# Linear attention into a Sinkhorn-routed mixture on one core: the emission table re-sorted, two small PSUM outputs moved within their bank

## The chip, the cores and the metric

The kernel runs on one core of a Trainium2 chip, in one launch. The metric is the device time of that core in microseconds (us), as the median of a few runs. Engines are named as the profile names them: PE multiplies matrices (PEld loads its weights), DVE and ACT work elementwise, POOL works elementwise and issues DMAs, SP issues DMAs. PSUM is the memory that PE writes to; it is cut into banks of 512 fp32 columns, and DVE and ACT read it.

## The reference

Linear attention over 8 batches, 8 heads, 576 positions and 64 dims, then an 8-expert layer whose routing weights come from Sinkhorn scaling. Cut to what matters:

```python
phi = lambda x: np.where(x > 0, x, np.exp(x) - 1.0) + 1.0
kv = einsum('bhsd,bhse->bhde', phi(k), v);  z = phi(k).sum(2)
att = einsum('bhsd,bhde->bhse', phi(q), kv) / (einsum('bhsd,bhd->bhs', phi(q), z)[..., None] + 1e-6)
x = att.transpose(0, 2, 1, 3).reshape(4608, 512)          # N = 4608 tokens
logits = x @ w_gate;  P = np.exp(logits - logits.max())   # N x 8
for _ in range(8):                                        # Sinkhorn
    P /= P.sum(1, keepdims=True) + 1e-9
    P /= P.sum(0, keepdims=True) + 1e-9                   # column sums over all tokens
    P *= N / E
out = sum over e of P[:, e:e+1] * (np.maximum(x @ w1[e], 0) @ w2[e])
```

## The kernel before, in words

**Work and stages.** Three stages overlap. The front makes attention for 16 pairs of batch and head group and writes `xT` (dims on partitions, tokens along the free side). The first expert, e = 0, starts as soon as tokens are there: 9 groups `g` of 512 tokens, each `relu(x @ w1) @ w2`. The other seven experts follow group by group (`unit`). From group 5 of expert 0 on, the first layer is done by `block7`, a seven-product scheme: for each half (`pair(0)`, `pair(1)`) PE makes products m1 to m7, each 4 matmuls 256 columns wide. Products m5 and m3 of a pair write one bank of the tile `att` ("att" in the profile), the others write `hq` and `Zye`. ACT copies parts of these products out (L767, L774, L781), DVE adds two of them and clips at zero (`addrelu`, the custom DVE instruction of L790, output `h`), ACT clips the other two (L784, L787). `unit_plain` then multiplies `h` by `w2` (L861, output `ye`).

**Sinkhorn.** While PE works on expert 0, DVE runs the 8 iterations of `sinkhorn`. One iteration is a chain of three steps: `f_a` on DVE (multiply, row sum, reciprocal, multiply, partial column sum `gs`; L503 to L510), `f_c` on PE (one small fp32 matmul with a matrix of ones, L515, which sums `gs` over the partitions into 8 columns of an `att` bank), `f_d` on DVE (`Dc` from those 8 columns, L519 the first time and L522 later, then a reciprocal, L524). The next `f_a` needs `f_d`. So does PE's next `f_c`, through the chain.

**Who shares what.** `att` is one PSUM tile `at2` of two banks. `att_bank()` hands out the banks in turn, for the router logits, for Sinkhorn's column sums and for the R bank of each `block7` pair:

```python
at2 = aps.tile([P, 2, 512], FP32, tag="att", name="att")
def att_bank():
    return at2[:, (len(p_att["order"]) - 1) % 2]
```

**What sets the order.** Each piece of work is a step with a number, added with its engine, a planned duration, dependencies and buffers. `_Plan.run` then calls the steps one after the other, and each call records its instructions. The first 1201 calls are written out by hand in `_FRONT` (a number, and a letter for the engine: p PE, a ACT, d DVE, g POOL, s SP, m a DMA's landing, n no engine). The rest is chosen greedily by planned time. The method `at` gives the planned start of a step on an engine; engine "none" stands for steps that only take a buffer. Every engine runs its own instructions in the order in which they were recorded.

**Where waits come from.** The recording layer adds the semaphore waits. When an instruction is recorded, it is made to wait for instructions of other engines recorded earlier whose accesses to the same tile conflict with its own. For `att` the programs show that it takes the two banks as one. In the program of before, the step that reads 8 column sums from columns 512 to 519 (second bank) waits for a matmul that writes columns 256 to 511 (first bank). Such a wait is called a cross-bank wait below. Its direction follows from the order of recording alone: the later recorded of the two waits. So the place of a step in `_FRONT` counts even between steps of different engines.

**Steps that the prediction names.** Sinkhorn's `f_c` are 512, 515, 518, 521, 524, 527, 530 and 533, its `f_d` are 513, 516 and so on to 534. 766, 780, 922, 988 and 1088 are m5 products, that is the first matmuls into an `att` bank; 767 is the ACT copy (L781) of 766's bank. 981 and 1052 are `f_h12`, the DVE step (L790) that reads a pair's finished `att` bank.

Of the kernel before, what the change touches and what calls it, by code (L numbers as in the profile page):

```python
# [17 lines left out]
class _Plan:  # L18
# [35 lines left out]
    def run(self):  # L54
# [10 lines left out]
        cfg = [0]  # L65

        def at(e, t, r):
            return max(free[e] + (self.TURN if e == "pe" and t["cfg"] != cfg[0] else 0.0), r)

        def slot(t):  # L70
# [64 lines left out]


_FRONT = """
    1n 2p 3p 4p 5p 102g 103m 6p 7p 8p 9p 10p 11p 12p 13p 14p 15p 16p 17p 18p 19p 20p 21p 117n 48s 49m 50g 51m 52g 53m
    75g 76m 106n 79g 80m 77g 78m 55d 54a 56d 124g 125m 0g 61n 126g 127m 62p 57n 22p 23p 24p 63a 107g 108m 64d 58p 59a
    65d 81a 25p 26p 27p 60d 66p 109g 110m 82d 83d 84n 28p 29p 151g 152m 111n 67a 153g 154m 88n 30p 31p 32p 68p 69a  # L140
    85p 86d 87a 89p 128g 129m 131d 71p 90a 70a 33p 583n 112g 113m 91d 34p 155g 156m 92d 114g 115m 35p 130a 36p 37p
    38p 39p 40p 41p 42p 43p 93p 44p 45p 72d 178g 179m 73p 74d 94a 46p 95p 96a 100p 137n 47p 116n 97a 132d 138p 584p
    180g 181m 182g 183m 585p 586p 587p 158d 101d 139a 98p 140d 99d 157a 164n 159d 165p 166a 133n 134p 135a 141d 118g
    119m 121g 122m 167d 588p 123n 160n 589d 590p 205g 206m 591d 168d 207g 208m 592p 136a 142p 161p 143a 144p 594p
    209g 210m 162d 234g 235m 236g 237m 145a 163d 596p 120n 169p 185d 146a 147p 597d 598p 600p 170a 171p 184a 148d
    599d 595d 149p 172a 602p 186d 191n 187n 238g 239m 192p 150d 188p 603d 593a 193a 606p 604p 189d 104g 105m 194d
    195d 173a 190a 176p 196p 177d 261g 262m 601a 605p 607p 612d 197a 211a 212d 213d 198p 174p 199a 608p 263g 264m
    200a 218n 219p 290g 291m 265g 266m 175d 220a 214n 221d 222d 215p 216a 620n 621p 217a 623p 622d 201p 292g 293m
    223p 202d 609p 241d 240a 614a 224a 624a 203p 225p 204d 625p 247n 226a 228p 227a 317g 318m 626a 232p 233a 267a
    627p 242d 243n 229d 248p 230p 629p 610p 268d 231d 244p 249a 250d 251d 296a 274n 319g 320m 344g 345m 630d 297d  # L150
    628a 616a 269d 275p 276a 277d 245a 611p 631p 321g 322m 270n 633p 278d 246a 252p 271p 632d 323a 253a 254p 272d
    346g 347m 634a 635p 641p 255a 273d 324d 653n 325d 348g 349m 371g 372m 256a 279p 280a 257p 258d 618d 654p 281p
    259p 303n 636a 655d 656p 282a 283a 294g 295m 260d 304p 284p 642p 305a 639p 657d 298d 285d 286p 306d 330n 649a
    331p 332a 287d 326n 307d 299n 300p 377a 402g 403m 301d 350a 658p 302d 333d 351d 660p 308p 327p 661d 334d 309a
    310p 328d 659a 311a 640p 400g 401m 378d 373g 374m 312a 662p 329d 315p 431g 432m 335p 352d 316d 664p 336a 313p
    337p 314d 637p 427g 428m 647a 338a 569d 663d 638p 357n 340p 358p 339a 341d 643p 359a 665d 342p 481g 482m 384n
    666p 360d 353n 343d 385p 361d 354p 386a 404g 405m 355a 645a 668p 356a 387d 644p 669a 362p 667d 570d 687p 363a
    670p 367p 364p 689p 456g 457m 651a 375g 376m 686n 672p 379d 571d 688a 365a 366a 406a 388d 368d 691p 548d 673p
    369p 370d 692a 407d 288p 680a 380n 381p 408d 413n 289a 433a 414p 676p 382d 572s 573m 415a 409n 454g 455m 549d
    487a 690a 383d 434d 416d 671p 677p 417d 555d 389p 410p 390a 391p 435d 693p 411d 429g 430m 412d 392a 393a 396p  # L160
    678d 550d 418p 419a 695p 397d 674p 420p 483g 484m 556d 557d 558s 559m 421a 394p 675p 395d 461d 440n 441p 694d
    696d 422a 436n 442a 437p 697p 699p 438d 458g 459m 485g 486m 439d 425p 443d 698a 398p 701p 426d 700a 444d 399a
    445p 423p 424d 488d 684a 682a 446a 460a 467n 720p 447p 452p 489d 703p 490g 448a 705p 462d 468p 702d 449a 719n
    463n 453d 706p 469a 450p 722p 470d 721a 538n 451d 495n 724p 496p 497a 551s 552m 471d 464p 704p 498d 560s 561m
    723a 465a 491n 466a 725d 726p 713d 574s 575m 499d 472p 473a 492p 493a 727d 474p 475a 494a 562d 563d 728p 476a
    711d 709p 500p 477p 576d 478d 501a 729d 710p 502p 503a 504a 479p 480d 707p 708p 505p 506d 730p 717d 577d 731d
    732p 507p 742p 508d 539g 540m 536n 756d 715a 734p 578d 763n 733a 757d 735d 752d 758d 759s 760m 509p 753d 754d
    736p 737p 510a 755d 537p 744a 511d 764p 808d 541g 542m 740p 778p 765a 553s 554m 768p 743p 543n 750d 770p 741p
    969s 970m 761s 762m 512p 769a 513d 748d 766p 771a 809d 810d 774p 544n 779a 780p 767a 781a 738p 772p 775d 514d
    784p 776p 786p 782p 785a 773d 579s 580m 788p 777a 787d 816p 783a 817a 739p 811s 812m 820p 789d 822p 515p 746a  # L170
    818p 790p 796p 819a 564d 565s 566m 567s 568m 516d 824p 517d 798p 823a 815n 799p 825d 797p 821a 518p 860d 791a
    830p 832p 806d 831a 826p 519d 861d 520d 836p 794p 837a 581s 582m 862d 827d 833a 1026s 1027m 804a 795p 840p 834p
    792p 841d 828p 829a 838p 839d 835a 793p 802d 868p 521p 870p 522d 842p 813s 814m 869a 800d 843a 523d 867n 545g
    546m 874p 912d 913d 871a 872p 873a 882p 863s 864m 846p 876p 883a 875a 888p 886p 889a 878p 524p 877d 848p 884p
    879d 885a 849p 847p 525d 854a 887a 914d 890p 880p 526d 547n 892p 850p 881a 893d 891d 527p 920p 856a 894p 844p
    895a 851p 845p 922p 858a 528d 529d 530p 852d 921a 926p 924p 927a 898p 923a 934p 928p 896p 919n 925a 915s 916m
    917s 918m 930p 935a 961d 531d 940p 941a 532d 899p 962d 897p 938p 906a 902p 929d 533p 931d 936p 937a 904a 534d
    939a 535d 944p 932p 942p 751a 943d 945d 745d 963d 903p 910d 933a 900p 865s 866m 946p 615d 972p 901p 954p 947a
    964d 973a 650d 974p 960n 978p 955p 908d 619d 975a 948p 965d 966d 959a 949p 979a 980p 976p 982p 681a 950p 971n
    613d 951p 652d 983d 648a 984p 986p 977a 956d 985a 987a 988p 952p 989a 992p 994p 967d 981d 968d 993a 995d 990p  # L180
    996p 1029p 712d 1031p 991a 1030a 714d 997d 953p 957d 998p 911d 1035p 1028n 1032a 1037p 958d 999a 1033p 1004p
    1000d 1036a 1005a 1006p 1001d 1009p 1039p 1034a 1002d 1003d 1014p 1007d 1008d 1040d 1010a 1012a 1038d 1015d 617a
    1016d 855d 1083s 1084m 679a 1017p 1041p 1043p 1045p 1020p 1044a 1046a 1049p 1051p 1042a 1022d 1047p 1050a 1021d
    1053p 1086p 646d 1048a 1088p 1018d 1052d 1054d 1087a 1023p 909d 1025d 1089a 1013g 1055p 1085n 1056a 1019d 1092p
    1093a 1024d 1094p 1011g 1057d 1090p 1061p 1058d 1063p 1062a 1066p 1059d 1064d 1065d 1060d 1096p 1097d 1140s 1141m
    718a 1091a 1095d 1067a 1068g 685d 1071p 1074p 1098p 1100p 1099a 1101a 1102p 1072d 1073d 1103a 1077p 1075d 1106p
    1107a 1108p 1104p 1110p 1143p 1078d 1145p 1079d 1069a 1080p 1105a 1142n 1070g 1111d 1144a 1112p 1109d 1149p 683a
    1146a 1082d 1197s 1198m 1113a 1076d 1081d 1114d 1115d 1116d 1117d 1150a 1151p 747d 1147p 1118p 1119a 1120p 1122d
    1121d 1123p 1153p 1154d 1128p 1131p 1155p 1157p 1159p 1130d 1133d 1124a 1129d 1152d 716a 1148a 749d 1158a 1160a
    1134p 1163p 1136d 1165p 1135d 1132d 1156a 1164a 1166d 1126a 1161p 1167p 1168d 1162a 1127g 1200p 1201a 1202p 1137p  # L190
    1203a 1169p 1170a 1139d 1138d 1206p 1207a 1208p 1204p 1175p 1171d 1172d 1176a 1177p 1180p 1199n 1205a 1173d 1174d
    1210p 1185p 1178d 1179d 1125g 1211d 1181a 1187d 1186d 1254s 1255m 1209d 1188p 1212p 1214p 1216p 1213a 1191p 1215a
    1217a
"""


@with_exitstack
def kernel(
    ctx: ExitStack,
    tc: tile.TileContext,  # L200
    q: bass.AP,
    k: bass.AP,
    v: bass.AP,
# [14 lines left out]
    NJ = S // PW  # L218
# [250 lines left out]
    def logits(b2):  # L469
        gl = S_.grp(p_att)  # L470

        def f_l(_):
            gl["tile"] = att_bank()[:, 0:NJ * E].rearrange("p (j e) -> p j e", e=E)
            for i in range(NJ):
                for c in range(NDT):
                    nc.tensor.matmul(gl["tile"][:, i, :], lhsT=xT[:, c, ts(NJ * b2 + i, P)], rhs=wg_sb[:, c, :],
                                     start=(c == 0), stop=(c == NDT - 1))
# [33 lines left out]
            gc = S_.grp(p_att)  # L511

            def f_c(_, gc=gc):
                gc["tile"] = att_bank()[:, 0:E]
                nc.tensor.matmul(gc["tile"], lhsT=ones_t, rhs=gs, start=True, stop=True)  # L515

            def f_d(_, it=it, gc=gc):
# [593 lines left out]
```

## Time and profile before

| | |
|---|---|
| median of 3 runs | 980.89 us (978.53, 980.89, 982.26) |
| the profiled execution's own time | 979.57 us |
| its span, first to last instruction | 977.8 us |
| PE busy | 959.2 us (98%), 8624 matmuls |
| DVE busy | 774.7 us (79%), 1481 instructions |
| ACT busy | 566.0 us (58%), 1004 instructions |
| POOL busy | 145.2 us (15%), 209 instructions |
| chain that ended last, by engine | PE 87%, DVE 6%, DMA 4%, ACT 1%, issue 1%, POOL 1% |
| column-sum matmuls (L515) | 8, each shown as two, 135.5 to 185.6 us |

PE's busy share holds little room, but a busy share tells nothing of the clock that PE was granted, and its gaps are not spread evenly. The bracket behind a row of the timeline is the idle time of the engine just before it and what ended that idle time. [...]

### The profile page before, as it was taken

To read this page: it belongs to the slowest core of one execution; us is meant where nothing else is said; L and a number is where in the kernel's file an instruction comes from. 1 tells how busy PE (TensorE), PEld (TensorE's weight loads), DVE (VectorE), ACT (ScalarE), POOL (GpSimd) and SP (SyncE) were. 2 spreads that over 40 slices of the span, in tenths; PEclk is the share of its full clock that TensorE was granted. 3 is DMA by queue.
4 is the path that set the end of the run, shared out by engine and by line. 5 is a ranking of instruction groups with operands and counts; after the bars stand their busy time and mean duration, and the time that the engine had idled before them with its cause. 6 is when DMAs were issued, how large, how long until landed. Compare 5 with 4: busy or idle time off the path is not lost.

```text
span 977.8 us, 21138 instructions
## 1 busy us (share of the span) xinstructions
PE 959.2 (98%) x8624; PEld 796.0 (81%) x8624; DVE 774.7 (79%) x1481; ACT 566.0 (58%) x1004; POOL 145.2 (15%) x209
## 2 busy tenths in 40 slices
PE   8999999899999999999999999999999999999998
PEld 4555566578888888888888888888888888888886
DVE  5897887778888788878888788878888788877775
ACT  6887744456555555555555555555555555555553
POOL 6441100001112111121112111121112111111110
PEclk9999999999999999999999999999999999999999
DMA  9997864012725422272225422272224422235554
GB/s 218 263 214 166 167 184 153 1 40 77 161 76 124 115 76 77 76 162 77 77 76 125 114 76 77 76 163 77 76 76 124 115 77 76 76 99 162 162 163 108
DMA packets 46193, 112.52 MB, mean 115 GB/s; under 512 B 4368, under 2 KB 26640, under 8 KB 46096
## 3 DMA queue, kind: packets, MB, share of 16 engines
q1 hardware_dynamic: 21056, 75.57, 23.6%
q0 software_dynamic: 24640, 35.07, 19.0%
q8 instruction: 67, 1.10, 0.4%
q10 hardware_dynamic: 400, 0.52, 0.2%
q14 instruction: 30, 0.25, 0.1%
HBM read 119.69 MB, written 17.69 MB: 141 GB/s over the span
## 4 chain that ended last, share of the span: by engine, by line
PE 87%; DVE 6%; DMA 4%; ACT 1%; issue 1%; POOL 1%; DVEq 0%; ACTq 0%; POOLq 0%
PE ye L979 32%; PE hq L755 23%; PE att L755 12%; PE Zye L755 6%; PE Zye L979 5%; PE ye L861 4%; DMA vv<-in_v_dram 2%; PE hq L633 2%; DMA w<-in_moe_w_dram 1%; DVE h L790 1%; DMA qin<-in_q_dram 1%; PE kv_ps L382 1%; PE att L409 1%; PE num_ps L432 0%; DVE W L919 0%
## 5 line engine op out<-in xcount | busy, mean ns | idle before, releaser
L993 DVE SCALAR_TENSOR_TENSOR acc<-ye,P_sb,acc 128x256 f32<-128x256 f32 x620 | 267.5, 479 | 124.8 <-PE ye L979 124.1
L755 PEld LDWEIGHTS <-W 128*128 128x128 f16 x2144 | 209.9, 98 | 29.7 <-issue 2.8
L979 PEld LDWEIGHTS <-S 128*128 128x128 f16 x1984 | 194.0, 98 | 23.9 <-DVE S L952 1.4
L1003 POOL TENSOR_TENSOR acc<-acc,st 128x256 f32<-128x256 f32 x124 | 88.0, 729 | 710.9 <-ACT st L1000 583.4
L979 PE MATMUL ye<-T,S 128*128 128x256 f16 x1488 | 192.8, 273 | 0.2 <-DVE S L952 0.2
L755 PEld LDWEIGHTS <-w 128*128 128x128 f16 x1608 | 157.7, 98 | 22.8 <-issue 2.8
L787 ACT ACTIVATE h<-hq 128x512 f16<-128x512 f32 x134 | 80.1, 598 | 150.9 <-PE hq L755 147.7
L979 PEld LDWEIGHTS <-h 128*128 128x128 f16 x1488 | 145.6, 98 | 17.4 <-issue 0.5
L755 PE MATMUL att<-xs,W 128*128 128x256 f16 x1008 | 151.2, 273 | 0.9 <-DVE h L790 0.8
L755 PE MATMUL hq<-xs,W 128*128 128x256 f16 x1008 | 151.2, 273 | 0.0
L755 PE MATMUL hq<-xs,w 128*128 128x256 f16 x1008 | 140.9, 273 | 0.9 <-DVE h L790 0.9
L784 ACT ACTIVATE h<-Zye 128x512 f16<-128x512 f32 x134 | 80.1, 598 | 40.1 <-PE Zye L755 40.1
L790 DVE CUSTOM_DVE_ANT_0 h<-att,s 128x512 f16<-128x512 f32 x126 | 86.6, 687 | 14.9 <-ACT s L774 10.0
L1000 ACT ACTIVATE st<-Zye,P_sb 128x256 f32<-128x256 f32 x124 | 52.3, 470 | 76.2 <-PE Zye L979 76.1
L952 DVE TENSOR_TENSOR S<-h 128x1024 f16<-128x1024 f16 x124 | 85.2, 687 | 10.9 <-ACT h L787 10.9
L774 ACT COPY s<-hq 128x512 f32<-128x512 f32 x126 | 73.5, 583 | 35.2 <-PE hq L755 35.1
L767 ACT COPY Zye<-hq 128x512 f32<-128x512 f32 x134 | 77.8, 581 | 25.5 <-PE hq L755 25.5
L790 DVE CUSTOM_DVE_ANT_0 h<-hq,s 128x512 f16<-128x512 f32 x126 | 86.6, 687 | 3.3 <-PE hq L755 3.0
L861 PE MATMUL ye<-w,h 128*128 128x512 f16 x312 | 76.8, 382 | 0.0
L781 ACT COPY s<-att 128x512 f32<-128x512 f32 x126 | 74.5, 591 | 3.4 <-PE att L755 2.3
L755 PE MATMUL Zye<-xs,w 128*128 128x256 f16 x504 | 75.6, 273 | 0.0
L979 PE MATMUL ye<-w,S 128*128 128x256 f16 x496 | 64.3, 273 | 0.7 <-DVE S L952 0.7
(102 smaller groups left out, 947.4 us busy)
## 6 DMA issues: line engine op xcount, KB each, us to landing
xs<-xd SPq DMA_DIRECT2D x63, 896.0 KB, 4.6
kin<-in_k_dram POOLq DMA_DIRECT2D x15, 576.0 KB, 8.5
out_dram<-acc SPq DMA_DIRECT2D x67, 128.0 KB, 2.4
w<-in_moe_w_dram POOLq DMA_DIRECT2D x16, 512.0 KB, 8.8
w<-in_moe_w_dram POOLq DMA_DIRECT2D x7, 1024.0 KB, 13.1
qin<-in_q_dram POOLq DMA_DIRECT2D x16, 288.0 KB, 7.4
vv<-in_v_dram POOLq DMA_DIRECT2D x16, 288.0 KB, 7.7
xd<-acc SPq DMA_DIRECT2D x5, 512.0 KB, 3.7
```

The costliest lines, as they stand in the source:

```text
L755: nc.tensor.matmul(dst[:, p, :], lhsT=lhs(p, c), rhs=rhs(c), start=(first and p == 0 and c == 0), stop=(c == 1), skip_group_check=True)
L767: nc.scalar.copy(out=Zt[1], in_=gX["tile"])
L774: nc.scalar.copy(out=gs2["tile"], in_=gX["tile"])
L781: nc.scalar.copy(out=gs5["tile"], in_=gR["tile"])
L784: nc.scalar.activation(out=hd(0, 0), in_=Zt[1], func=AF.Relu)
L787: nc.scalar.activation(out=hd(1, 0), in_=gX["tile"], func=AF.Relu)
L790: nc.vector._custom_dve(TENSOR_ADD_SAT, out=dst, in0=ps, in1=sb, s0=3.0e38, s1=0.0)
L861: nc.tensor.matmul(gy[tt]["tile"], lhsT=gh["tile"][:, f, ds(P * tt, P)], rhs=gw2["tile"][:, f, :], start=(f == 0), stop=(f == NFT - 1))
L952: nc.vector.tensor_tensor(out=Sx[:, i], in0=a0, in1=a1, op=op)
L979: nc.tensor.matmul(bank(g_)[:, s, :], lhsT=lhs(s, kk), rhs=rhs(kk), start=(new and s == 0 and kk == 0), stop=(kk == 3), skip_group_check=True)
L993: nc.vector.scalar_tensor_tensor(out=dst(), in0=bank(g_)[:, s, :], scalar=P_sb[:, gg, e:e + 1], in1=dst(), op0=ALU.mult, op1=ALU.add)
L1003: nc.gpsimd.tensor_tensor(out=dst(), in0=dst(), in1=gst["tile"], op=ALU.add)
```

## The change

Three edits.

1. In `_Plan.run`, `at` returns the ready time for engine "none", so that buffer-only steps no longer queue behind each other in the plan.
2. The logits and the column sums are written 16 fp32 columns further into their bank (columns 16 on, in place of 0 on).
3. The 1201 entries of `_FRONT` are put in another order, that of their planned times. The sequence of each engine's own entries (p, a, d, g, s) stays exactly as it was; what changes is how the engines' sequences are interleaved, and the places of some m and n entries.

```diff
         def at(e, t, r):
+            if e == "none":
+                return r
             return max(free[e] + (self.TURN if e == "pe" and t["cfg"] != cfg[0] else 0.0), r)
...
-            gl["tile"] = att_bank()[:, 0:NJ * E].rearrange("p (j e) -> p j e", e=E)
+            gl["tile"] = att_bank()[:, 2 * E:2 * E + NJ * E].rearrange("p (j e) -> p j e", e=E)
...
-                gc["tile"] = att_bank()[:, 0:E]
+                gc["tile"] = att_bank()[:, 2 * E:3 * E]
```

The new order, shown where the prediction uses it (stretches of the table, one step's neighbours each):

```
Sinkhorn's first column sums, 512p, their reader 513d, and the m5 products behind them
 before: 512p 769a 513d 748d 766p 771a 809d 810d 774p 544n 779a 780p 767a
 after:  512p 766p 513d 774p 767a 748d 780p
the sixth, 527p and 528d
 before: 527p 920p 856a 894p 844p 895a 851p 845p 922p 858a 528d 529d 530p
 after:  527p 891d 920p 894p 528d 844p 529d 895a 851p 845p 858a 921a 922p 852d 919n 530p
after Sinkhorn, the R bank's reader 981d and the next pair's m5, 988p
 before: 988p 952p 989a 992p 994p 967d 981d
 after:  981d 986p 985a 988p
and once more, 1052d and 1088p
 before: 1088p 1018d 1052d 1054d
 after:  1052d 1088p
```

Laid side by side, the two programs hold the same instructions in the same order on each of the five engines. Apart from the column offset they differ in the semaphores waited for by 39 instructions, 13 on PE, 16 on DVE and 10 on ACT. With edit 2 alone, no wait differs from before.

More of the change, by code (lines that the diff above doesn't have):

```diff
@@ L137 @@
 _FRONT = """
[L138 to L192, printed above, removed]
+    1n 102g 103m 117n 106n 583n 48s 49m 2p 3p 50g 51m 4p 52g 53m 5p 6p 75g 76m 7p 8p 79g 80m 9p 10p 77g 78m 55d 54a
@@ new lines @@
+    11p 12p 124g 125m 13p 14p 15p 0g 16p 56d 17p 18p 126g 127m 19p 20p 21p 61n 107g 108m 62p 109g 110m 22p 63a 23p
+    24p 57n 151g 152m 58p 64d 65d 25p 59a 26p 81a 27p 153g 154m 60d 82d 66p 28p 29p 67a 83d 30p 128g 129m 31p 32p 68p
+    84n 85p 69a 88n 112g 113m 89p 86d 87a 90a 71p 131d 155g 156m 33p 34p 35p 70a 36p 91d 37p 38p 114g 115m 39p 40p
+    92d 130a 41p 42p 43p 72d 93p 178g 179m 44p 94a 45p 73p 46p 74d 137n 95p 111n 180g 181m 96a 132d 100p 47p 97a 138p
+    182g 183m 158d 584p 139a 101d 585p 586p 118g 119m 157a 587p 140d 98p 99d 164n 165p 133n 121g 122m 159d 134p 166a
@@ new lines @@
+    141d 205g 206m 588p 135a 167d 590p 136a 592p 589d 160n 207g 208m 142p 591d 161p 143a 168d 116n 209g 210m 144p
+    162d 594p 145a 163d 596p 234g 235m 185d 146a 169p 597d 147p 598p 170a 148d 236g 237m 600p 184a 599d 595d 171p
+    238g 239m 149p 172a 602p 186d 191n 593a 150d 187n 192p 620n 603d 188p 193a 120n 104g 105m 606p 189d 173a 194d
+    604p 195d 190a 601a 176p 123n 261g 262m 196p 177d 605p 197a 607p 612d 211a 263g 264m 212d 198p 174p 199a 608p
+    213d 218n 290g 291m 200a 175d 219p 265g 266m 214n 215p 220a 621p 216a 221d 292g 293m 217a 240a 623p 222d 622d
@@ new lines @@
+    201p 614a 223p 609p 202d 224a 241d 624a 203p 225p 247n 625p 204d 317g 318m 226a 242d 228p 227a 232p 243n 627p
+    626a 229d 233a 267a 268d 248p 230p 249a 319g 320m 629p 231d 274n 344g 345m 296a 610p 250d 321g 322m 251d 244p
+    628a 616a 630d 275p 297d 611p 276a 346g 347m 269d 348g 349m 631p 270n 245a 277d 371g 372m 246a 633p 323a 278d
+    252p 632d 271p 253a 634a 254p 272d 294g 295m 635p 255a 273d 324d 641p 256a 653n 325d 279p 257p 280a 654p 258d
+    636a 281p 618d 259p 282a 656p 655d 303n 326n 283a 260d 304p 657d 284p 305a 402g 403m 298d 642p 400g 401m 285d
@@ new lines @@
+    639p 649a 306d 286p 330n 287d 299n 331p 307d 300p 332a 373g 374m 658p 301d 377a 302d 660p 333d 350a 351d 308p
+    327p 661d 309a 334d 659a 310p 431g 432m 640p 328d 311a 378d 427g 428m 662p 312a 329d 481g 482m 352d 315p 335p
+    664p 316d 336a 647a 313p 337p 314d 357n 637p 338a 569d 638p 339a 663d 340p 358p 341d 665d 643p 359a 342p 666p
+    360d 384n 353n 343d 385p 361d 354p 386a 668p 404g 405m 355a 387d 645a 456g 457m 644p 356a 667d 669a 375g 376m
+    570d 362p 379d 686n 687p 363a 571d 651a 670p 388d 572s 573m 688a 367p 364p 689p 365a 672p 366a 691p 406a 368d
@@ new lines @@
+    673p 548d 692a 380n 369p 680a 288p 370d 413n 407d 381p 289a 433a 408d 454g 455m 414p 382d 409n 549d 676p 415a
+    429g 430m 383d 434d 483g 484m 671p 487a 416d 677p 417d 690a 389p 555d 410p 390a 435d 391p 411d 693p 392a 412d
+    678d 396p 393a 418p 550d 695p 419a 397d 674p 556d 420p 557d 394p 421a 675p 558s 559m 395d 440n 436n 551s 552m
+    422a 461d 441p 560s 561m 694d 437p 442a 696d 574s 575m 697p 438d 458g 459m 439d 485g 486m 699p 443d 698a 425p
+    700a 398p 426d 444d 701p 399a 684a 682a 445p 719n 423p 446a 720p 424d 467n 460a 447p 488d 452p 703p 490g 489d
@@ new lines @@
+    448a 538n 544n 539g 540m 705p 462d 449a 541g 542m 702d 463n 468p 545g 546m 453d 706p 469a 450p 721a 722p 470d
+    495n 491n 451d 724p 471d 496p 464p 497a 704p 723a 498d 465a 726p 725d 466a 713d 472p 492p 499d 473a 727d 474p
+    493a 728p 562d 475a 494a 563d 709p 476a 711d 500p 576d 477p 501a 710p 478d 502p 729d 479p 503a 707p 480d 504a
+    708p 505p 715a 730p 506d 732p 717d 577d 507p 731d 733a 742p 508d 734p 536n 756d 509p 763n 578d 757d 736p 735d
+    510a 752d 737p 758d 753d 759s 760m 537p 744a 553s 554m 764p 754d 740p 765a 755d 778p 511d 768p 743p 769a 770p
@@ new lines @@
+    741p 808d 771a 779a 750d 512p 766p 513d 774p 767a 748d 780p 809d 738p 781a 810d 775d 772p 543n 784p 514d 776p
+    785a 786p 777a 782p 788p 783a 816p 739p 773d 817a 969s 970m 787d 761s 762m 820p 746a 815n 822p 789d 515p 818p
+    564d 579s 580m 516d 790p 819a 811s 812m 517d 796p 565s 566m 823a 567s 568m 821a 824p 791a 798p 581s 582m 799p
+    825d 797p 860d 1026s 1027m 813s 814m 806d 518p 830p 832p 519d 831a 861d 826p 520d 836p 794p 837a 833a 795p 804a
+    840p 862d 834p 827d 863s 864m 792p 841d 828p 838p 829a 793p 839d 835a 802d 868p 867n 521p 870p 869a 522d 842p
@@ new lines @@
+    800d 874p 843a 523d 872p 871a 882p 873a 846p 883a 876p 875a 888p 886p 912d 889a 878p 913d 524p 848p 877d 879d
+    884p 849p 525d 885a 914d 526d 915s 916m 847p 917s 918m 890p 854a 880p 887a 865s 866m 892p 881a 850p 893d 856a
+    527p 891d 920p 894p 528d 844p 529d 895a 851p 845p 858a 921a 922p 852d 919n 530p 926p 961d 924p 927a 531d 898p
+    923a 532d 925a 934p 928p 935a 896p 547n 930p 940p 962d 899p 941a 929d 931d 897p 906a 938p 902p 533p 936p 534d
+    944p 937a 535d 932p 904a 942p 939a 903p 943d 751a 945d 900p 933a 745d 946p 963d 972p 947a 910d 901p 973a 615d
@@ new lines @@
+    964d 954p 971n 960n 650d 974p 908d 978p 975a 619d 955p 965d 948p 966d 959a 613d 979a 949p 652d 681a 980p 648a
+    976p 982p 977a 950p 983d 956d 951p 967d 984p 981d 986p 985a 988p 968d 987a 952p 989a 992p 994p 993a 990p 995d
+    996p 991a 1029p 712d 1031p 714d 1030a 953p 997d 1032a 957d 998p 1028n 911d 1035p 999a 1083s 1084m 958d 1037p
+    1036a 1033p 1000d 1004p 1001d 1006p 1002d 1005a 1034a 1009p 1003d 1007d 1039p 1008d 1010a 1014p 1012a 1040d 617a
+    1038d 1017p 679a 1013g 1015d 1041p 1016d 1011g 1043p 855d 1045p 1044a 1020p 1046a 1042a 1049p 1022d 1051p 1021d
@@ new lines @@
+    1050a 1047p 646d 1053p 1018d 1048a 1086p 1052d 1088p 1087a 1054d 1023p 1089a 909d 1055p 1025d 1085n 1092p 1019d
+    1056a 1140s 1141m 1094p 1024d 1093a 1090p 1057d 1061p 1058d 1063p 1059d 1062a 718a 1066p 1064d 1091a 1065d 1096p
+    1060d 1067a 1071p 1097d 1068g 1074p 1095d 685d 1098p 1072d 1100p 1073d 1099a 1102p 1075d 1101a 1077p 1103a 1106p
+    1078d 1108p 1079d 1107a 1104p 1069a 1110p 1105a 1070g 1143p 1111d 1145p 1144a 1109d 1080p 683a 1112p 1146a 1142n
+    1082d 1149p 1076d 1197s 1198m 1113a 1151p 1081d 1150a 1147p 1114d 1118p 1115d 1120p 1116d 1119a 1117d 1123p 747d
@@ L193 @@
+    1153p 1122d 1124a 1128p 1121d 716a 1154d 1148a 1131p 1130d 1155p 1133d 1157p 1129d 1159p 1152d 1158a 1134p 1160a
+    749d 1156a 1163p 1136d 1165p 1135d 1164a 1161p 1132d 1126a 1167p 1166d 1162a 1127g 1200p 1168d 1202p 1201a 1125g
+    1137p 1203a 1169p 1139d 1199n 1206p 1138d 1170a 1254s 1255m 1208p 1207a 1171d 1204p 1175p 1172d 1177p 1173d 1176a
+    1205a 1174d 1180p 1178d 1179d 1210p 1181a 1185p 1211d 1188p 1187d 1186d 1212p 1209d 1214p 1213a 1216p 1215a 1191p
     1217a
```

## The prediction

> **What bounds the kernel now.** I read the page first: PE is busy 98% of the span, so only PE's gaps and the clock it gets can give time. The table of busy time by stretch then says where both lie.
>
> ```profile
> 130.00:225.00 95.00, 88.00 (x628) 61.51 (x626) 73.44 (x161) 46.20 (x84) 2.14 (x3) 0.98 0.31 102
> 225.00:977.80 752.80, 747.20 (x6809) 665.76 (x6807) 598.45 (x1151) 422.57 (x793) 98.98 (x139) 1.00 0.37 103
> 173.40:176.80 3.40, 0.59 (x6) 0.56 (x7) 3.23 (x8) 0.00 (x0) 0.00 (x0) 1.00 0.00 0
> 176.90:180.20 3.30, 3.30 (x14) 1.76 (x12) 0.45 (x1) 1.58 (x3) 0.00 (x0) 0.50 0.02 5
> ```
>
> Columns: window, length, busy time of PE, PEld, DVE, ACT, POOL (with counts), granted clock, DMA. From 130 to 225 us, where Sinkhorn and the first `block7` groups run, PE is idle 7.0 of 95 us; in the 753 us behind it, 5.6. Inside that stretch PE is nearly empty for one window, and in the next it has half the clock. The waits of PE in that stretch name who holds it:
>
> ```profile
> PE att L515 <- DVE gs L510: 3.3, 1, 3.3
> PE att L515 <- DVE h L790: 1.6, 2, 1.4
> PE att L755 <- DVE h L790: 0.8, 1, 0.8
> PE hq L755 <- DVE h L790: 0.6, 1, 0.6
> PE att L755 <- ACT acc L781: 0.3, 1, 0.3
> PE att L755 <- DVE Dc L519: 0.3, 1, 0.3
> ```
>
> (total us, times, longest.) All are small PE steps behind DVE or ACT. The timeline shows why DVE is late although it is idle itself:
>
> ```profile
> 168.62 0.39 PE L515 MATMUL att<-gs,ones_t 128*128 128x8 f32 x2 [1.39 <-DVE h L790]
> ...
> 172.32 0.60 PE L755 MATMUL att<-xst,W 128*128 128x256 f16 x4
> 172.96 0.16 DVE L522 SCALAR_TENSOR_TENSOR Dc<-Dc,att 128x8 f32<-128x8 f32 x1 [4.40 <-PE att L755]
> ...
> 175.70 0.45 DVE L510 TENSOR_REDUCE gs<-wt 128x8 f32<-128x288 f32 x1
> 176.07 0.68 DVE L310 COPY acc<-ye 128x512 f32<-128x512 f32 x1
> 176.21 0.39 PE L515 MATMUL att<-gs,ones_t 128*128 128x8 f32 x2 [3.28 <-DVE gs L510]
> ...
> 202.05 0.69 DVE L790 CUSTOM_DVE_ANT_0 h<-att,s 128x512 f16<-128x512 f32 x1 [2.83 <-PE att L755]
> 203.99 0.60 PE L755 MATMUL att<-xs,W 128*128 128x256 f16 x4 [0.77 <-DVE h L790]
> ```
>
> The column sums of 168.62 are ready at about 169, but their reader `Dc` starts only at 172.96: it waits for the m5 product of 172.32, which is in the other bank. Sinkhorn's chain then runs alone for 3.2 us (172.96 to 176.15) while PE stands before the next column sums.
>
> **The change, part by part.** A matmul's successor normally starts 0.109 us (256 columns) or 0.216 us (512) after it, but the bracket counts from its modelled end (0.273 or 0.379 us); so a stall costs its bracket plus 0.16. I keep a running shift of PE, negative for earlier.
>
> *The column offset.* No wait depends on it. Price by the nearest rows: `Dc` took 0.155 us from column 0 of the first bank and 0.163 to 0.165 from column 0 of either bank later; L993 reads the second half of a bank as fast as the first (0.48). Bounds -0.1 to +0.1 us; I take 0.
>
> *The "none" steps.* They issue no instruction and the engines' orders are unchanged: 0. No DMA, SP or POOL entry moves on its queue.
>
> *Sinkhorn's first column sums (766p ahead of 513d, 767a ahead of 780p).* 766 no longer waits for `Dc`: bracket 0.29, by starts 0.43 (136.09, where 0.14 after the column sums of 135.52 is usual). In exchange `Dc` waits for 766's end, about 136.27, and 780 waits for 767: `Dc` to 136.47, ACT copy 0.58 to about 137.08, 780 starts at 137.12, 0.16 later than before. But ACT is then one copy ahead, and the wait at 138.72 (bracket 0.30) goes: 138.42. Shift -0.30.
>
> *Second to fourth reader.* `Dc` at 144.91 stood 1.20 us behind an ACT copy of the other bank; now it waits for PE work that ends 0.9 earlier. So the L790 step that PE awaits at 148.78 (bracket 0.20, stall 0.36) is done in time. Shift -0.66.
>
> *Fifth reader and sixth sums, 168.62.* `Dc` at 163.99 loses its 0.7 us wait for ACT (0.1 stays), so `gs` ends 1.28 earlier, at 166.1; and 527 no longer waits for the L790 step recorded behind it, which ended at 168.56. PE is free for it at 166.41. The stall of 1.39 + 0.16 = 1.55 goes. Shift -2.21. Were only the second of these true, `gs` at 167.37 would leave 0.3.
>
> *Sixth reader, 176.21.* 528 now stands ahead of 922. `Dc` starts when its column sums and the two L790 steps before it are done, 167.41; the chain of 3.2 us ends at 170.61, and PE gets there at 172.76 - 2.21 = 170.55. Of 3.28 + 0.16 = 3.44 us, 0.1 stays. Shift -5.55. The cover is the PE work from 168.86 to 172.7 (before), 3.9 us against a chain of 3.2; without it the chain is back on the path with 3.2.
>
> *The half clock.* 14 matmuls ran in 3.41 us at 0.50 (176.87 to 180.28): in full four of 256 columns, four of 512 and four of 256, which are 8 x 0.109 + 4 x 0.216 = 1.74 us at full clock. It follows the one nearly empty window; with that filled I take the loss to go: 1.67 more. Its other bound is 0.
> [...]
>
> *Seventh and eighth.* `Dc` at 181.01 (idle 3.66 before it) comes earlier and gives DVE slack; PE itself had no stall there. `Dc` at 186.97 stood 0.95 for an ACT copy; now it waits for the matmuls ahead of that copy (185.71 + 0.60), and DVE gains some 0.4 on PE. PE's start at 189.60, 0.26 late behind its eight L861 matmuls (187.62 + 8 x 0.216) because of L790, is then in time. Shift -5.81.
>
> *After Sinkhorn (981d ahead of 988p, 1052d ahead of 1088p).* DVE's 981 stood idle 2.83 us for the next pair's product in the other bank. Now it follows its predecessor at once, and 988 waits for it instead. On the clock of before, 981 would run from 199.20 (198.54 + 0.66) to 199.89, and 988 was due at 199.57: it loses 0.31, and with it all that is queued behind it on PE, L861 first. But the stalls at 203.99 (0.77 + 0.16) and 205.38 (0.09) end, since DVE is no longer late there: -0.72. The same at 1052: idle 1.06 gone, 1088 due at 216.29 loses 0.34, the stall at 218.38 (0.61 + 0.16 = 0.77) goes: -0.43. Shift -6.96. The bad end of this term is the two new waits with no gain, +0.65 in place of -1.15.
>
> Behind 225 us no wait differs, and PE's remaining stalls (0.9, 0.4 and 0.3 in its waits) stay as they are.
>
> Sum: 6.96 + 1.67 = 8.63 us. Against the profiled execution's 979.57 that is 970.9. The runs shown lie around it (978.53, 980.89, 982.26; with the profiled one a mean of 980.31); from that mean I take **971.7**. A measurement of this kernel can tell about 0.5%, 4.9 us, from no change.
>
> **The rivals.**
> *The clock does not come back (973.4).* For: the one profiled execution shows the half clock once, starting 0.67 us after PE was back, so it may depend on how the stall falls in time; the runs spread by 3.7 us, and the median one may not have had it. Against: the only stall of over 2 us came just before it. 971.7 + 1.67. [...]
>
> *DVE holds PE at the new waits (976.0).* For: DVE is busy 73.4 of 95 us here, and if 981 were kept until its old place in DVE's time, 988 would lose 3.1 and 1088 1.5 us in place of 0.31 and 0.34: 971.7 + 3.95, and a little DVE lag carried on. Against: DVE's 2.83 us before 202.05 are idle, and it was PE that ended them.
>
> *No effect (980.3).* The waits between the banks differ in the programs, but if others end last (the true inputs of `Dc` and L790) nothing moves. Against: the column sums end 4 us before their reader starts, and nothing else runs on DVE.
>
> *Slower (990).* The turned direction, PE waiting for DVE's `h` instead of DVE for PE, recurs in each later unit at the 0.34 of 1088: 55 units cost 18.7, and from 26 units on (8.63 / 0.34) the gain is gone. For: the last two places that the change touches, 988 and 1088, both have that new wait. Against: the later units' waits are unchanged, and the row of 225 to 977.8 stays in its order.
>
> **How the numbers follow.** Forecast 0.62, clock 0.18, DVE 0.13, no effect 0.05, slower 0.02. The forecast and the clock case lie over 0.5% faster; the DVE case sits on that bound of 975.4 to 976, and I give half of it to each side: faster 0.87, same 0.11, slower 0.02. The range runs from the fastest run shown less the sum and the small unknowns (978.53 - 8.63 - 0.9 = 969.0) to just under the DVE case, 975.6, which leaves out somewhat under 2 in 10.
>
> **What would show it.** Right: `Dc` of the sixth iteration starts before its m5 product, PE has no wait for L515 over 0.3 us, the granted clock is 1.00 throughout 130 to 225, that stretch ends about 8.6 us earlier, and two new PE waits of about 0.15 (brackets) for L790 stand before L755 at about 192 and 208 us. Wrong: an idle bracket over 1 us before 988 or 1088, a row at 0.50, or `Dc` still idle for PE's `att` at L755.

## The result and the profile after

The changed kernel takes 971.60 us, the median of 4 executions (970.76 to 972.00), where the kernel before takes 979.71 us, the median of 4 (977.99 to 982.26). The ratio is 0.9914, 95% interval 0.9888 to 0.9940. The prediction was 971.7, faster.

The busy time by stretch, after (columns as in the prediction: window, length, busy time of PE, PEld, DVE, ACT and POOL with counts, granted clock, DMA share, GB/s):

```profile
91.60:94.80 3.20, 3.20 (x32) 1.79 (x27) 2.18 (x5) 1.40 (x2) 1.60 (x3) 0.50 0.64 195
...
130.00:216.40 86.40, 85.58 (x640) 60.96 (x637) 73.71 (x162) 46.40 (x85) 1.85 (x3) 1.00 0.34 112
216.40:970.20 753.80, 748.22 (x6819) 666.63 (x6816) 599.37 (x1153) 422.63 (x793) 99.32 (x140) 1.00 0.37 102
```

From 130 us to the end of the changed stretch PE is idle 0.8 of 86.4 us, at clock 1.00; behind it 5.6 us, as before. The first row shows something that the profiled execution of before does not have: a half clock in the front, where PE's waits are the same in both programs. It puts PE 1.1 us further back in this execution. PE's waits in the changed stretch (total, times, longest):

```profile
PE att L757 <- ACT acc L783: 0.4, 1, 0.4
PE att L757 <- DVE h L792: 0.2, 1, 0.2
```

None of the six waits of before is left: the two lines have names that occur in the list of before, but stand at other places. The first line is the new wait of 780 for the ACT copy, the second that of 1088 for `h`; the one of 988 shows only in the starts (+0.30 us). The timeline around the sixth and seventh column sums:

```profile
167.59 0.28 PE L517 MATMUL att<-gs,ones_t 128*128 128x8 f32 x2
...
168.52 0.15 DVE L524 SCALAR_TENSOR_TENSOR Dc<-Dc,att 128x8 f32<-128x8 f32 x1
168.60 2.75 PE L863 MATMUL ye<-w,h 128*128 128x512 f16 x12
...
171.19 0.60 PE L757 MATMUL att<-xst,W 128*128 128x256 f16 x4
171.27 0.45 DVE L512 TENSOR_REDUCE gs<-wt 128x8 f32<-128x288 f32 x1
...
171.78 0.39 PE L517 MATMUL att<-gs,ones_t 128*128 128x8 f32 x2
```

`Dc` (L524 here, L522 before) now starts 0.9 us behind its column sums instead of 4.3, with no idle time of DVE before it, and 2.7 us ahead of the m5 product (171.19) that it used to wait for. Its chain ends with `gs` at 171.7, and PE, busy with twelve L863 matmuls and m5 meanwhile, starts the next sums at once.

### The profile page after: what moved, and what is told of

Same layout as the page of the kernel before. It is cut to its first block, busy times and chain, and to the rows that moved or that the text cites. A ratio compares the mean times of both kernels' runs of the same rounds, so it can differ in the third digit from the quotient of the medians.

```text
span 970.2 us, 21138 instructions
## 1 busy us (share of the span) xinstructions
PE 957.8 (99%) x8624; PEld 796.5 (82%) x8624; DVE 774.8 (80%) x1481; ACT 566.0 (58%) x1004; POOL 145.6 (15%) x209
## 4 chain that ended last, share of the span: by engine, by line
PE 90%; DMA 4%; DVE 3%; ACT 1%; issue 1%; POOL 1%; DVEq 0%; ACTq 0%; POOLq 0%
PE ye L981 33%; PE hq L757 23%; PE att L757 12%; PE Zye L757 6%; PE ye L863 6%; PE Zye L981 5%; DMA vv<-in_v_dram 4%; PE hq L635 2%; PE kv_ps L384 1%; DMA kin<-in_k_dram 1%; DVE h L792 1%; PE att L411 1%; DVE acc L995 1%; PE att L434 1%; PE num_ps L434 1%
## 5 line engine op out<-in xcount | busy, mean ns | idle before, releaser
L863 PE MATMUL ye<-w,h 128*128 128x512 f16 x312 | 76.7, 382 | 0.3 <-DMA w<-in_moe_w_dram 0.2
```

The costliest lines, as they stand in the source:

```text
L863: nc.tensor.matmul(gy[tt]["tile"], lhsT=gh["tile"][:, f, ds(P * tt, P)], rhs=gw2["tile"][:, f, :], start=(f == 0), stop=(f == NFT - 1))
```

## The experiments

Each ran beside the kernel before on the same chip, in three batches on three chips. Line numbers shift by a few lines from kernel to kernel. A "mean" below is over all executions of a kernel, whatever the chip; the kernel before ran 45 times beside the experiments, with a mean of 980.32 us (980.12, 980.58 and 980.21 by batch), the changed kernel or one with the same waits 16 times, with a mean of 971.41.

**Columns against order.** `move_only` is the kernel before with edit 2 alone, that is the line of the column sums below and the same shift for the logits. `order_only` is the changed kernel with both shifts taken back:

```diff
-                gc["tile"] = att_bank()[:, 0:E]
+                gc["tile"] = att_bank()[:, 2 * E:3 * E]
```

> Only the column offset of the column sums and the logits; the table and the planner as before. Theory (the table's order decides, through the waits between the two banks of `att`): no wait differs, so the time of before, ratio 1.000 within 0.002, `Dc` of the sixth iteration again about 4 us behind its column sums. Rival (the edge of the bank costs something by itself): each of the eight column sums and two logits steps cheaper, and if that were the whole gain, the ratio is 0.991 and `Dc` is shorter than the 0.155 to 0.165 us of before.

> The new table and the "none" steps, with column sums and logits back at the first columns of their banks. Theory: all of the gain, ratio 0.9914 (971.6 against 979.7), stalls as in the changed kernel. Rival (address): the time of before, 1.000; a mixture would lie between.

Measured: `move_only` 981.02, ratio 1.0002 (0.9990 to 1.0014); `order_only` 971.44, ratio 0.9913 (0.9899 to 0.9926). The offset is worth nothing that these intervals show, and the order everything. The programs with and without edit 1 have the same instructions and waits on every engine, so edit 1 is nothing beside the table.

**One step.** `one_528` records the sixth reader 528 ahead of the m5 product 922 and leaves all else as before:

```diff
-    527p 920p 856a 894p 844p 895a 851p 845p 922p 858a 528d 529d 530p
+    527p 920p 856a 894p 844p 895a 851p 845p 528d 922p 858a 529d 530p
```

`undo_528` is the changed kernel with that step, and the next one on DVE, put back:

```diff
-    527p 891d 920p 894p 528d 844p 529d 895a 851p 845p 858a 921a 922p 852d 919n 530p
+    527p 891d 920p 894p 844p 895a 851p 845p 858a 921a 922p 528d 529d 852d 919n 530p
```

> One step of the table: 528 (the sixth reader, `Dc` and `cc`) recorded ahead of 922 (the m5 product), all else as before. Theory (terms add): the stall of 176.21 goes and nothing else, -3.4 us; with the half clock 1.7 more where it followed from that stall: 974.6 with it, 976.3 without, ratio 0.9948 or 0.9965, and the stall of 1.39 at 168.62 stays. Rival (the stalls hang on each other, so that one without the others is given back later): DVE is then late at the next places (L790 before 189.60, L510 before 185), and the time is within 1 us of before.

> The changed kernel with 528 and 529 (the sixth reader and the next DVE step) recorded behind the m5 product 922 again. Theory (terms add): the changed kernel's 971.5 plus 3.35 for the stall before the seventh column sums, which starts at about 172.8, and 1.3 on the mean for the half clock behind it, so 974.9 to 976.2, ratio 0.9948 to 0.996; a row at 0.50 behind the stall in most executions. Rival (the half clock is not tied to this stall): 974.9 with a clock of 1.00 there. Rival (the stall is absorbed since the steps around it are early now): 971.5 to 973, ratio 0.992.

Measured: `one_528` 975.49, ratio 0.9953 (0.9939 to 0.9968); `undo_528` 976.16, ratio 0.9951 (0.9937 to 0.9965). Compared matmul by matmul with the profile of before, PE in `one_528` comes 3.45 us earlier at 176.21 and about 1.7 more where the half clock was, and all but 0.2 of it is left at the end of the span. First the two longest of PE's waits in `one_528` from 130 to 226 us:

```profile
PE att L513 <- DVE h L788: 1.6, 2, 1.4
PE att L753 <- DVE h L788: 0.8, 1, 0.8
```

then those of `undo_528`:

```profile
PE att L515 <- DVE gs L510: 3.3, 1, 3.3
PE att L755 <- ACT acc L781: 0.4, 1, 0.4
PE att L755 <- DVE h L790: 0.2, 1, 0.2
```

One stall is taken from a list, or put back into one, and the others stay as they were. So this term adds to the others, whether they are there or not. The half clock came back with the stall in `undo_528`:

```profile
173.00:176.00 3.00, 1.32 (x7) 1.08 (x8) 2.86 (x8) 0.00 (x0) 0.00 (x0) 0.58 0.00 0
176.00:179.50 3.50, 3.50 (x14) 1.90 (x13) 3.29 (x8) 1.58 (x3) 0.00 (x0) 0.50 0.02 5
```

**Half of the table.** `early_only` is the kernel before with the new order up to step 535, `late_only` with the new order behind it. One stretch of each:

```diff
-    512p 769a 513d 748d 766p 771a 809d 810d 774p 544n 779a 780p
+    512p 766p 513d 774p 767a 748d 780p
```

is among the changes of `early_only`, and

```diff
-    988p 952p 989a 992p 994p 967d 981d
+    981d 986p 985a 988p
```

among those of `late_only`.

> The new order of the table up to the eighth reader (535), the old one behind it, columns and planner as before. Theory: -5.8 us from the waits and about -1.3 on the mean from the half clock, 972.6, ratio 0.9925 to 0.993; no wait of 0.15 for L790 at about 192 and 208, but 0.77 and 0.61 before the products of 198 and 212. Rival (the whole gain is there, the late part trades evenly): the changed kernel's 971.5, ratio 0.9914.

> The old order up to the eighth reader, the new one behind it (981 ahead of 988, 1052 ahead of 1088). Theory: -1.14 us (+0.31 -0.94 -0.09, +0.34 -0.77), half clock as before: 978.8, ratio 0.9988. Rival (DVE holds PE at the new waits, since Sinkhorn's late part has not come forward): 988 and 1088 lose 3.1 and 1.5 us, 984, ratio 1.004. Rival (even trade): 979.95, ratio 1.000.

Measured: `early_only` 973.17, ratio 0.9920 (0.9907 to 0.9933), 1.7 us above the changed kernel in the mean, of which the late steps account for 1.2 in its trace. Its waits of PE in the stretch:

```profile
PE att L753 <- DVE h L788: 0.8, 1, 0.8
PE hq L753 <- DVE h L788: 0.6, 1, 0.6
PE att L753 <- ACT acc L779: 0.4, 1, 0.4
```

The waits for `h` of after-Sinkhorn that the late half removes are still there. `late_only` took 979.65, ratio 0.9992 (0.9981 to 1.0002), so its time alone can't tell its 1.1 us from nothing. Its trace can: PE shifts by +0.31, -0.94, -0.09, +0.33 and -0.77 at the five places, -1.16 in sum. The price of 3.1 us at 988 is refuted.

**The half clock by itself.** `fill_stall` is the kernel before with idle matmuls in the stall:

```diff
             def f_c(_, it=it, gc=gc):
+                if it == 6:
+                    for _ in range(13):
+                        nc.tensor.matmul(att_bank(), lhsT=warm[:, 0:P], rhs=warm, start=True, stop=True)
```

> The kernel before, with 13 idle matmuls of 512 columns (13 x 0.216 = 2.8 us) put in front of the seventh column sums, into their own bank: they start when `Dc` has been read at 172.96 and end 0.3 us ahead of the sums, so the stall of 3.28 us keeps its length and PE is busy in it. The matmuls add nothing to the result, since the sums overwrite them. Theory (the nearly empty window of the stall brings the half clock behind it): no row at 0.50 between 176 and 183 us and fewer runs under a clock of 0.998, the stall still there; 978.2 to 979, ratio 0.998 to 0.9985. Rival (the half clock comes from something else, such as the load of the hour): half-clock rows as often as before, 979.95, ratio 1.000. Rival (the matmuls run at half clock or late and hold the sums): slower by up to 2.8, ratio 1.003.

Measured: 977.81, ratio 0.9968 (0.9955 to 0.9980), all 6 executions between 977.52 and 977.98 at a clock of 0.999 or 1.000. Its timeline shows the stall filled, and its length unchanged:

```profile
172.83 0.16 DVE L525 SCALAR_TENSOR_TENSOR Dc<-Dc,att 128x8 f32<-128x8 f32 x1 [4.40 <-PE att L758]
173.04 2.96 PE L516 MATMUL att<-warm 128*128 128x512 f16 x13 [0.25 <-DVE Dc L525]
...
176.09 0.39 PE L518 MATMUL att<-gs,ones_t 128*128 128x8 f32 x2
```

The same three windows, first of `move_only` (the waits of before), then of `fill_stall`:

```profile
173.00:176.00 3.00, 0.00 (x0) 0.00 (x0) 2.76 (x8) 0.00 (x0) 0.00 (x0) 0.96 0.00 0
176.00:179.50 3.50, 3.31 (x13) 2.07 (x14) 1.33 (x3) 1.58 (x3) 0.00 (x0) 0.50 0.00 0
179.50:183.00 3.50, 3.50 (x14) 1.87 (x13) 0.87 (x4) 0.57 (x1) 0.00 (x0) 0.56 0.02 5
```

```profile
173.00:176.00 3.00, 2.96 (x13) 1.17 (x12) 2.77 (x8) 0.00 (x0) 0.00 (x0) 1.00 0.00 0
176.00:179.50 3.50, 3.41 (x26) 2.49 (x26) 1.49 (x5) 2.15 (x4) 0.00 (x0) 1.00 0.02 5
179.50:183.00 3.50, 3.50 (x24) 2.16 (x22) 3.29 (x9) 1.17 (x2) 0.00 (x0) 1.00 0.01 2
```

With 0.00 us of PE work in the first window, the two behind it have the clock at 0.50 and 0.56; with 2.96 us of work that nobody needs, both have 1.00. In all 13 profiles it is so: the 4 with the stall empty (before, `move_only`, `undo_528`, `late_only`) have the half clock behind it, the 9 with the stall gone or filled have none between 130 and 225 us. So the empty stall brings the half clock, though not in every execution (see "The half clock" in the next section). Its price was larger than the 1.67 us of the one execution that I had seen: in `move_only` and `undo_528` it lasts twice as long. From the means it is 980.32 - 977.80 = 2.5 us, of which up to 0.5 may be the half clock of the front (below), since these 6 executions were hardly touched by that either.

**The tie of the banks itself.** `split_before` keeps the old table and the old columns. From the closing of the front on, the two banks are two tiles (`apx` is the stack that now holds the pool of `at2`). They are the same two banks of PSUM as before. `split_after` does the same to the changed kernel.

```diff
-        return at2[:, (len(p_att["order"]) - 1) % 2]
+        i = (len(p_att["order"]) - 1) % 2
+        return atl[i] if atl else at2[:, i]
...
         front.close()
+        apx.close()
+        ap2 = ctx.enter_context(tc.tile_pool(name="ap2", bufs=1, space=PSUM))
+        atl.extend(ap2.tile([P, 512], FP32, tag=f"at{i}", name=f"at{i}") for i in range(2))
```

> The kernel before, with its old table and old columns, but from the closing of the front on the two banks of `att` are two PSUM tiles, so that no wait ties one bank to the other; in which order steps of different banks are recorded then no longer matters. Theory (the new order gains only by turning waits between the banks): it gains what the change gains and also loses the new waits of it (0.59 at 136.96, 0.31 at 199.57, 0.34 at 216.29) and some small stalls that both kernels have (0.2 at 154.46, 0.2 at 162.74, 0.2 at 187.18, about 0.3 at 240 to 241): -9.3 us, and -1.7 where the half clock goes with the nearly empty window, so 968.7 to 970.4, ratio 0.989 to 0.9905, at or below the changed kernel. Rival (the order in the table matters by itself, not the tie of the banks): the time of before, 979.7, ratio 1.000. Rival (closing the pool and opening another adds a wait in the front): PE has a new wait of some us at about 95 us and the gain is smaller by it.

> The changed kernel with the two banks of `att` as two PSUM tiles from the closing of the front on: new table, new columns. Theory (the table and the columns act only through the tie of the banks): the same as the kernel before with two tiles, 969.0, ratio 0.989, though the orders differ. Rival (the new order is worth something by itself): below it by up to the change's 8 us. Rival (it costs something by itself): between 969.0 and the changed kernel's 971.5.

> The changed kernel once more, beside the two with split banks. Theory: 971.5, ratio 0.9914, no row at 0.50 between 130 and 225 us, in about half of the executions one at 91.5 to 95; slower than the split kernels by 2.2 to 2.7 us, of which the three new waits are 1.25 (0.6, 0.3, 0.34). Rival (the scatter hides that difference): within 1 us of them.

Measured: `split_before` 969.04, ratio 0.9890 (0.9876 to 0.9904); `split_after` 968.37, ratio 0.9879 (0.9861 to 0.9896); the changed kernel beside it 971.00, ratio 0.9909 (0.9893 to 0.9925). With split banks the two tables give the same program but for the column offset, so the difference of the first two is scatter; their 9 executions have a mean of 968.86, 2.5 us below the changed kernel. The intervals of the ratios overlap, but the ranges of the times do not: 967.59 to 970.36 against 970.52 to 972.72. The busy time by stretch of `split_before`:

```profile
130.00:214.00 84.00, 84.00 (x648) 60.75 (x645) 73.01 (x162) 46.06 (x85) 1.42 (x2) 1.00 0.35 115
214.00:968.60 754.60, 748.66 (x6825) 667.24 (x6823) 599.90 (x1154) 423.40 (x794) 99.81 (x140) 1.00 0.37 102
```

PE is busy for 84.00 of 84.00 us, and the list of its waits is empty from 130 to 226 us. Matmul by matmul against `after_again`, `split_after` gains 0.60 at 136.75, 0.20 at 191.79 and 0.33 at 207.82, which are the three new waits, then 0.25 at the seventh column sums, and 1.2 in small steps (153.33, 161.60, 179.35, 230.77 to 244.22) that the list of waits is too coarse to name. This version beats both kernels.

**The front.** In the front PE stands 1.1 to 1.2 us for a transfer, behind 36 router matmuls of 8 columns, ahead of the half clock seen there. `split_fill` adds 4 idle matmuls to `split_before`, in that gap at 90 us.

```diff
             gkv["tile"] = kvps.tile([P, 2, 512], FP32, tag="kv", name="kv_ps")
+            if n == 11:
+                for _ in range(4):
+                    nc.tensor.matmul(gkv["tile"][:, 0, :], lhsT=warm[:, 0:P], rhs=warm, start=True, stop=True)
```

> The kernel before with two tiles, and 4 idle matmuls of 512 columns (4 x 0.216 = 0.86 us) ahead of the key-value products at 90.87, into their own bank, where PE stands 1.1 us for a DMA of `vv`; the products overwrite them. Half the profiles so far had a row at 0.50 at 91.5 to 95 us, whatever the kernel. Theory (that half clock too follows from the stretch with little for PE to do, here 36 matmuls of 8 columns and then the stall): clock 1.000 in nearly all executions and the scatter down to some 0.5 us; 968.6, ratio 0.9885. Rival (the half clock in the front has another cause): half of the executions at 0.998 to 0.999, 969.0. Rival (the idle matmuls hold the products): up to 0.9 us slower, 970.

Measured: 968.82, ratio 0.9884 (0.9867 to 0.9901); 4 executions from 968.61 to 969.30, at 0.999 to 1.000. That is no faster than split banks alone, and 4 executions don't show that the half clock is gone. Inconclusive.

## Why the prediction was right

The shift of PE by step, in us, from the start of each matmul in the profiles of after and before:

| step of the prediction | predicted | measured |
|---|---|---|
| column offset, "none" steps | 0 | 0 (`move_only` 1.0002) |
| first column sums: stall, new wait of 780, old wait at 138.72 | -0.43 +0.59 -0.46 | -0.43 +0.60 -0.46 |
| second to fourth reader, 148.78 | -0.36 | -0.36 |
| fifth reader and sixth sums, 168.62 | -1.55 | -1.55 |
| sixth reader, 176.21 | -3.34 | -3.29 |
| half clock | -1.67 | -1.67 in this pair; -1.7 in the means |
| seventh and eighth, 189.60 | -0.26 | -0.26 |
| after Sinkhorn, 988 | +0.31 -0.93 -0.09, taken as -0.72 | +0.30 -0.94 -0.09 |
| the same, 1088 | +0.34 -0.77 | +0.33 -0.77 |
| sum | -8.63 | -8.87, of which -0.3 in drifts of 0.1 and less |

The reason held, and `split_before` shows it: without the tie of the banks the old order costs nothing. The order only chose which of two instructions in different banks waits, and the prediction could price each because the work that would cover a turned wait was in the trace. PE's 3.9 us from 168.86 to 172.7 did hide Sinkhorn's chain of 3.2: all but 0.15 of that stall's 3.44 us went.

**The half clock** was the term with the weakest ground, one row of one execution, and its size came out right by luck: the prediction took the loss of that row in every execution. The executions of before, `move_only` included, have a granted clock of 1.000 in 11 of 57 (mean 978.14), 0.998 in 12 (979.54), 0.996 or 0.997 in 24 (980.95) and 0.994 in 10 (982.14). So some have none, as the rival said, and many lose more than the 1.67 us of that row; the mean of the two happens to be near it. After, 6 of 16 are at 1.000 (970.91), and none below 0.997. Between executions at 1.000 the change is worth 978.14 - 970.91 = 7.2 us, against 6.96 of shifts; the clock adds 2.2 us of loss before less 0.5 after, 1.7 in the mean. The 0.5 that stays is the half clock in the front, in 5 of 13 profiles, whatever the kernel; in the profiled execution of after PE is 1.3 us behind at 130 us, most of it from that, so that of the 8.87 the span shows only 7.6.

That it follows from the empty stall was an estimate from that one row; `fill_stall` shows it, with the clock at 1.00 behind 2.96 us of idle matmuls in 3.00 where `move_only` had 0.50 behind 0.00 us of work. PE did not stand still in all of the time ahead of it: in the profile of before it was busy for 0.59 of the 3.40 us from 173.40 to 176.80, and the clock fell at 176.87. In `undo_528` PE was busy for still more of it; the 3.41 us up to the fall of the clock and the 3.41 behind it:

```profile
170.09:173.50 3.41, 1.30 (x8) 0.59 (x6) 1.86 (x7) 1.07 (x2) 0.00 (x0) 1.00 0.00 0
173.50:176.91 3.41, 2.23 (x11) 1.74 (x12) 3.27 (x8) 0.73 (x2) 0.00 (x0) 0.50 0.00 0
```

So in this execution the half clock came behind 3.41 us with 1.30 us of PE work. How little PE must do for it, and why the same stall brings it in some executions and not in others, no run here shows.

**The rivals.** The clock came back in the stretch (1.00 from 130 to 216.40 us), so 973.4 fell. DVE did not hold PE at 988 and 1088 (0.30 and 0.33), nor in `late_only`, where Sinkhorn had not come forward. "No effect" fell with the result and with `order_only`. The slower case fell with the last row of the table: behind 219 us PE's shift in the profile of after stays within 0.1, and the new direction does not recur.

The forecast kept the tie of the banks as given. The larger gain was there: the tie cost 11.5 us in the means (980.32 - 968.86, half clock included), of which the order recovers 8.9. Part of the rest is the three new waits that the prediction counted as the price of the new direction.

The split kernels show what guarding the two banks as one cost, these 11.5 us; what an access without any guard does, no run here shows.

## What to carry to other kernels

When an engine waits although its true inputs are long done, look at which instruction released it: if that one works in another bank of the same tile, first give the banks tiles of their own, and only then think about order; here that was worth 2.5 us more than the order, and left the order without effect. The stall of PE of 3.3 us cost more than its length here, since the half clock behind it added 2.0 to 2.5 us in the mean; where such a stall can't be removed, idle matmuls into a bank that the next product overwrites can be tried, which took that part away here (`fill_stall`, 977.80 against 980.32 in the means). Price a turned wait by the work that stands beside it in the trace; the terms of this kernel, each read from one row of the trace before, came to 8.63 where 8.87 was measured.

## What was not expected of the hardware

The half clock behind the stall lasted 3.4 us in the profiles of before and `late_only`, and 6.8 us in those of `move_only` and `undo_528`, with the same stall of 3.3 us. The traces differ in when the clock fell: 0.66 us behind PE's return from the stall (before) and 0.2 us ahead of it (`late_only`), against 0.4 us (`move_only`) and 1.2 us ahead of it (`undo_528`). So it was long in the two profiles where it began 0.4 us or more ahead of PE's return, and short in the other two; four events do not show where the bound lies, or whether there is one. The half clock at 91.5 to 95 us came in 5 of 13 profiles and comes behind 36 matmuls of 8 columns and a stall of 1.2 us; whether these cause it stays open after `split_fill`.
